# Three more groups of attention scores in float16 pairs, and casts moved from VectorE and ScalarE to GpSimd

## The chip, the cores and the metric

The kernel runs on one core of one Trainium2 chip. A core has a matrix engine (TensorE, PE in the rows, its weight loads PEld), three engines that work on 128 partitions at a time (VectorE DVE, ScalarE ACT, GpSimd POOL) and a queue that issues transfers (SyncE, SP). Each engine works through its own list of instructions in order and waits on semaphores for the others. The metric is the device time of one execution in microseconds (us); less is better.

## The reference

```python
# q, k, v: 8 batches, 12 heads, 448 positions, head size 64, all float32
scores = scale * np.matmul(q, k.transpose(0, 1, 3, 2)) - np.log(S)
attn = 1.0 / (1.0 + np.exp(-scores))
attn_out = np.matmul(attn, v)                       # heads side by side: x is 3584 x 768
gate = 1.0 / (1.0 + np.exp(-(x @ w_gate)))          # w_gate, w_val: 768 x 1536
val = x @ w_val
out = (gate * val) @ w_out                          # w_out: 1536 x 768
```

The weights come as float64 bits of which the kernel makes float32 itself.

## The kernel before, in words

**Attention.** The loop runs over 24 groups m (8 batches times 3 sets of four heads) and, in each, over seven *beats* g, one for each block of 64 keys: 168 beats. In a beat PE computes the scores of that block (L542, in `scores`), ACT applies the sigmoid (L557), and PE multiplies the scores of two beats before with the values (L572). `values` and ACT's copy (L582) give x, which goes to DRAM.

A group's scores are made in one of two ways. In float32, a beat has 8 score matmuls. *In halves* (`in_halves(m)`, before: m odd and from 3 on, eleven groups), each of q and k is split into a high and a low float16 part, and a beat has 12 float16 matmuls. The split is `split_qk(m)`, in three steps. Step one, two groups ahead at beat 0: DVE takes the largest magnitude (L503) and bounds it (L505). Step two, at beat 4: PE sums it over partitions with matmuls behind the next beat's scores (L548), and ACT copies the sum (L559, tile `qka`). Step three, one group ahead at beat 0: DVE makes a power of two (L511, L512), the two high parts (L516), the two low parts (L518) and the factor for the sigmoid (L520, L521). The halves lie in one tile `hl` with one buffer.

**Beside it.** `convert` makes float16 pairs of Strassen-like combinations of the weights, one `step` at a time. For a block of weights (four chunks of 128 x 384, eight steps) DVE takes the magnitude (L216), POOL limits it (L199, `limit`), DVE assembles the float32 (L205, L206, L213) and takes its largest value (L111). Then seven operands: sums of chunks (L261), a cast to the high part (`cast`), DVE's low part (L231, `split`, `lag` steps later) and the store (`send`). During attention the first six blocks (FIRST) are converted, with POOL's casts (L379, `scaled_gpsimd`, one multiplication) and DVE's sums; PACE says which share of the 50 chunk steps is due by which beat. From group 7 on the first x is loaded back (`load_x`), subtracted by DVE (L347, `subtract_x`) and split (`split_x`): a cast (L376 on ACT or L382 on DVE) and DVE's rest (L390), 21 times.

**After attention** come eight visits of the first two layers: each tick is a product of nine matmuls (L719). In the first visit, ticks 2 to 32, the last two blocks of the first part are converted (`in_first` = 2, scales w30 and w31): ACT takes magnitudes (L219), POOL makes the sums (L261), DVE the casts (L382) and the low parts (L231). POOL also multiplies gates with values (L929) and subtracts for the next x (L347). The scale of a block is spread over partitions by one PE matmul (L687) of a tile `each` that DVE makes (L120). The rest of the weights and the output layer follow.

The order on each engine is the order in which the program is written; nothing reorders it.

Of the kernel before, what the change touches and what calls it, by code (L numbers as in the profile page):

```python
# [9 lines left out]
F32 = mybir.dt.float32  # L10
F16 = mybir.dt.float16
# [16 lines left out]
TINY = 2.0 ** -100  # L28
BF16_MAX = 3.3895313892515355e38

PACE = (0, 0), (77, 0.6), (146, 1)

AHEAD, AHEAD_FF = 3, 3

X_LAG, X_BESIDE = 5, 6

SUM_MAX = 2.0 ** 119

# [21 lines left out]
def sigmoid_attention_glu_kernel(ctx: ExitStack, tc: tile.TileContext, qk, v, wg, wv, wo, out):  # L60
# [157 lines left out]
    def magnitude_scalar(to, bits):  # L218
        nc.scalar.activation(to, bits.bitcast(F32), AF.Abs)  # L219

    def convert(words, parts, ks, largest_of, cast, lag, drain_after, adder=nc.gpsimd):

        pool = words.pool

        unsummed, unsplit, unsent, todo, now = [], [], [], {}, 0

        def split():

            while unsplit and unsplit[0][0] + lag <= now:
                _, x, sc, hl, where = unsplit.pop(0)  # L230
                nc.vector.scalar_tensor_tensor(out=hl[:, 1], in0=x, scalar=sc.s, in1=hl[:, 0], op0=ALU.mult, op1=ALU.subtract)  # L231
                unsent.append((hl, where))

        def send():

            while unsent:
                hl, (key, sends) = unsent.pop(0)
                for d in sends(hl):
                    nc.sync.dma_start(**d)
                stored.add(key)  # L240

        def high(x, sc, where):
            hl = pool.tile([P, 2, CW], F16, tag="whl", name="whl", bufs=words.held)
            cast(hl[:, 0], x, sc.s)
            unsplit.append((now, x, sc, hl, where))

        def to_a(jp, t, n):
            return ("a", jp, t, n), lambda hl: [dict(out=a_dram[jp][t][n], in_=hl)]

        def to_op(k, n):  # L250
            return ("o", k, n), lambda hl: [dict(out=o_ops[n][:, :, k, a].rearrange("o p f -> p o f"),
                                                 in_=hl[:, a].rearrange("p (o f) -> p o f", f=P)) for a in range(2)]

        def operands(fs, sc, to):
            a11, a12, a21, a22 = fs
            for x, n in ((a22, 6), (a11, 0), (a12, 4)):
                yield lambda x=x, n=n: high(x, sc, to(n))
            s2 = pool.tile([P, CW], F32, tag="wf4", name="wf", bufs=1)

            def summed(n, x, y, z, op):  # L260
                adder.tensor_tensor(out=x, in0=y, in1=z, op=op)  # L261
# [24 lines left out]
        groups = [(w_scales[jp, t], lambda n, jp=jp, t=t: to_a(jp, t, n), True) for jp, t in parts]
        groups += [(o_scales[k], lambda n, k=k: to_op(k, n), False) for k in ks]
        def value(at, i):
            if at < len(groups) and i < 4:
                value_of[at, i] = pool.tile([P, CW], F32, tag=f"wf{i}", name="wf", bufs=3)  # L290
                words.begin(value_of[at, i])
                return True

        value_of = {}
        for at, (sc, to, everywhere) in enumerate(groups):
            if at == drain_after:
                yield from drain()
            if at in (0, drain_after):
                step(lambda: value(at, 0))
                yield  # L300
                step(words.limit)
                yield
            for i in range(4):
                f = value_of[at, i]
                next_ = (at, i + 1) if i < 3 else (at + 1, 0)
                begun = []

                def first():
                    if next_[1] or next_[0] != drain_after:
# [12 lines left out]
                yield
            fs = [value_of.pop((at, i)) for i in range(4)]
            scale = sc.steps() if everywhere else [sc.row_powers]
            for i, f in enumerate(scale):
                todo.setdefault(now + 1 + i, []).append(f)
            for i, f in enumerate(operands(fs, sc, to)):
                todo.setdefault(now + len(scale) + (0 if everywhere else 1) + i, []).append(f)
        yield from drain()

    def convert_steps(n_groups, everywhere, lag):
        return 8 * n_groups + lag + (TAIL + 4 if everywhere else TAIL)
# [43 lines left out]
        nc.scalar.activation(to, x, AF.Copy, scale=s)  # L376

    def scaled_gpsimd(to, x, s):
        nc.gpsimd.tensor_scalar(out=to, in0=x, scalar1=s, scalar2=None, op0=ALU.mult)  # L379

    def scaled_vector(to, x, s):
        nc.vector.tensor_scalar(out=to, in0=x, scalar1=s, scalar2=None, op0=ALU.mult)  # L382

    casts = itertools.chain((scaled_vector,) * X_BESIDE, itertools.cycle((scaled, scaled_vector)))

    def scaled_in_turn(*args):
        next(casts)(*args)
# [95 lines left out]
    with tc.manual_schedule(), tc.tile_pool(name="att", bufs=2) as att, tc.tile_pool(name="sc", bufs=2, space=PSUM) as scp, \  # L483
# [8 lines left out]
                nc.sync.dma_start(out=loads[m].rearrange("r p t s -> r p (t s)"), in_=qk[m // NQ, m % NQ])  # L492

        def in_halves(m):
            return 1 < m < B * NQ and m % 2 == 1

        def split_qk(m):

            x = loads[m]
            each = att.tile([P, 2], F32, tag="qkm", name="qkm", bufs=1)  # L500
            told = att.tile([P, 2], BF16, tag="qkt", name="qkt", bufs=1)
            total = att.tile([P, 2, 2], F32, tag="qka", name="qka", bufs=1)
            nc.vector.tensor_reduce(out=each, in_=x.rearrange("r p t s -> r t p s"), axis=AX.XY, op=ALU.max,  # L503
                                    apply_absolute_value=True)
            nc.vector.tensor_scalar(out=told, in0=each, scalar1=SUM_MAX, scalar2=TINY, op0=ALU.min, op1=ALU.max)  # L505
# [5 lines left out]
            nc.vector.tensor_tensor(out=m_, in0=total[:, 0], in1=total[:, 1], op=ALU.add)  # L511
            nc.vector.tensor_scalar(out=s_.bitcast(U32), in0=m_.bitcast(U32), scalar1=EXPONENT, scalar2=EXPONENT,  # L512
                                    op0=ALU.bitwise_and, op1=ALU.bitwise_xor)
            hl = att.tile([P, 2, 2, 2, S], F16, tag="hl", name="hl", bufs=1)
            for t in range(2):
                nc.vector.tensor_scalar(out=hl[:, 0, t], in0=x[:, :, t], scalar1=s_[:, t:t + 1], scalar2=None, op0=ALU.mult)  # L516
            for t in range(2):
                nc.vector.scalar_tensor_tensor(out=hl[:, 1, t], in0=x[:, :, t], scalar=s_[:, t:t + 1], in1=hl[:, 0, t],  # L518
                                               op0=ALU.mult, op1=ALU.subtract)
            nc.vector.tensor_scalar(out=inv.bitcast(U32), in0=m_.bitcast(U32), scalar1=EXPONENT, scalar2=None, op0=ALU.bitwise_and)  # L520
            nc.vector.tensor_scalar(out=back, in0=inv[:, 0:1], scalar1=inv[:, 1:2], scalar2=scale / 4, op0=ALU.mult, op1=ALU.mult)  # L521
# [8 lines left out]
        def scores(m, g):  # L530
# [6 lines left out]
            for i, (kt, qt) in enumerate(((1, 0), (0, 1), (0, 0)) if in_halves(m) else ((None, None),)):  # L537
                for h in range(2):
                    for p in range(2):
                        qs, ks_ = (x[halves[h], qt, 0, p], x[halves[h], kt, 1, p, ks]) if in_halves(m) else \  # L540
                            (x[halves[h], p, 0], x[halves[h], p, 1, ks])
                        nc.tensor.matmul(sc[halves[p], h, :S], lhsT=ks_, rhs=qs, start=i == 0, stop=i == 2 or not in_halves(m))  # L542
            sums = qk_sums[:1]
# [64 lines left out]
                                         rhs=bias[halves[h]].to_broadcast([HP, S]), start=True, stop=True)  # L608

        load_first()  # L610
        warm_up(3)
        ones = const.tile([P, HP], BF16, name="ones")
        nc.vector.memset(ones, 2.0 ** (1 - TOP))
        words = Words(att, chunks(halves_of_jps[:FIRST], ()), AHEAD, 6, magnitude_vector)
        weights = convert(words, halves_of_jps[:FIRST], (), max_abs, scaled_gpsimd, 2, None, nc.vector)
        n_chunks, n_weights, done = 8 * FIRST + 2, convert_steps(FIRST, True, 2), 0

        def due_at(beat):
# [442 lines left out]

    in_first = 2 * len(JPS_OF_PARTS[0]) - FIRST
    words = Words(conv, chunks(halves_of_jps[FIRST:], range(KH)), AHEAD_FF, 4, magnitude_scalar)
    weight_casts = itertools.chain((scaled_vector,) * (N_OPS * in_first), itertools.repeat(scaled))
    weights = convert(words, halves_of_jps[FIRST:], range(KH), sum_abs, lambda *args: next(weight_casts)(*args), 1, in_first)
    n_first = convert_steps(in_first, True, 1)
    n_chunks = 8 * (2 * JPS - FIRST - in_first + KH) + 2
    n_all = n_chunks - 2 - 8 * KH + convert_steps(KH, False, 1)
    calm = [t for v_ in range(1, n_a - 1) for t in range(starts[v_] + 2, starts[v_] + 25 if v_ < 3 else starts[v_ + 1] + 2)]
    due = {}  # L1070
    last = n_all - n_chunks
# [51 lines left out]
```

## Time and profile before

| what | us |
|---|---|
| median of 3 runs (lowest, highest) | 1116.47 (1115.51, 1117.61) |
| the profiled execution's own time | 1115.85 |
| its span, first to last instruction | 1113.8 |
| busy: PE, DVE, ACT, POOL | 1103.7, 764.6, 675.7, 427.9 |

The profile's page gives, for each engine, busy time and its share of the span, then forty equal slices of 27.8 us with the busy share in tenths, the chain of work that ended last, and the costliest groups of instructions. A row of the timeline reads: start, length, engine, line, operation, output and inputs, count, and in brackets how long the engine had been idle before it and what ended that wait.

### The profile page before, as it was taken

Reading aid. Unit: us, or ns where it says so; the run is one execution under the profiler, and the core shown is the slowest. Engines: PE = TensorE matmul, PEld = TensorE weight load, DVE = VectorE, ACT = ScalarE, POOL = GpSimd, SP = SyncE. Lnnn points to the kernel's source line nnn. Section 1 sums busy time; section 2 is a strip of 40 time slices with the busy share of each in tenths; the row PEclk is TensorE's granted clock in tenths of the full one; section 3 lists DMA queues with packets and bytes.
Section 4 is the critical chain, followed back from the end, with each engine's and each line's share of the span. In section 5 each row is a group of like instructions: output and inputs, shape, how many; then the busy total and the mean of one; then the engine's idle time right before and its main releaser. Section 6 shows DMA issues by size and latency. Waiting matters only on the chain.

```text
span 1113.8 us, 21314 instructions
## 1 busy us (share of the span) xinstructions
PE 1103.7 (99%) x7642; PEld 556.7 (50%) x7642; DVE 764.6 (69%) x1292; ACT 675.7 (61%) x1278; POOL 427.9 (38%) x371
## 2 busy tenths in 40 slices
PE   9999999999999999999999999999999999999998
PEld 3444444445455555555555555555555555555554
DVE  3769999966974465566567766675339687676863
ACT  6888788887566665866566667665445354253330
POOL 0032323352541342342234433333266193672940
PEclk9999999999999999999999999999999999999999
DMA  8779699779788556843656899898756876867644
GB/s 313 261 237 362 237 311 324 239 268 346 260 283 284 184 177 224 277 125 95 200 176 221 267 360 270 267 288 210 236 156 203 254 229 209 270 202 247 189 127 141
DMA packets 174538, 265.34 MB, mean 238 GB/s; under 512 B 49248, under 2 KB 151264, under 8 KB 174432
## 3 DMA queue, kind: packets, MB, share of 16 engines
q1 hardware_dynamic: 174144, 263.60, 73.4%
q8 instruction: 60, 0.98, 0.4%
q14 instruction: 46, 0.38, 0.1%
q10 hardware_dynamic: 288, 0.38, 0.1%
HBM read 182.48 MB, written 81.43 MB: 237 GB/s over the span
## 4 chain that ended last, share of the span: by engine, by line
PE 93%; DVE 5%; DMA 1%; issue 0%; ACT 0%; DVEq 0%; SPq 0%
PE un L719 76%; PE av L572 9%; PE sc L542 8%; DVE whl L231 1%; DMA wraw<-wv 1%; DVE qkm L503 1%; DVE x0c L111 0%; DVE hl L518 0%; PE sc L607 0%; DVE xt L347 0%; DVE wf L206 0%; DVE hl L516 0%; DVE wf L213 0%; DVE whl L382 0%; DVE wf L205 0%
## 5 line engine op out<-in xcount | busy, mean ns | idle before, releaser
L719 PEld LDWEIGHTS <-A 128*128 128x128 f16 x3024 | 295.5, 98 | 275.8 <-issue 0.7
L719 PE MATMUL un<-b,A 128*128 128x448 f16 x1512 | 296.6, 352 | 0.0
L719 PE MATMUL un<-b,v 128*128 128x448 f16 x1512 | 296.5, 352 | 0.0
L719 PE MATMUL un<-hh,A 128*128 128x448 f16 x1008 | 273.0, 352 | 0.0
L719 PEld LDWEIGHTS <-v 128*128 128x128 f16 x1512 | 147.7, 98 | 137.5
L719 PE MATMUL un<-hl,A 128*128 128x448 f16 x504 | 177.6, 352 | 0.0
L572 PE MATMUL av<-a,v 64*64 64x448 f32 x1344 | 157.2, 538 | 0.0
L199 POOL TENSOR_SCALAR wf<-wf 128x384 f32<-128x384 f32 x72 | 41.9, 582 | 230.4 <-ACT wf L219 126.2
L929 POOL TENSOR_TENSOR g<-c,g 128x448 f32<-128x448 f32 x44 | 59.3, 1348 | 177.9 <-DVE c L702 79.6
L557 ACT ACTIVATE a<-sc,bias 128x896 f32<-128x896 f32 x91 | 91.6, 1008 | 33.2 <-PE sc L542 30.7
L702 DVE TENSOR_TENSOR c<-un,u 128x448 f32<-128x448 f32 x72 | 44.8, 623 | 83.7 <-PE un L719 76.4
L914 ACT ACTIVATE g<-c,back 128x448 f32<-128x448 f32 x72 | 48.1, 668 | 78.9 <-DVE c L702 75.7
L557 ACT ACTIVATE a<-sc,bias,qkb 128x896 f32<-128x896 f32 x77 | 84.9, 1105 | 13.1 <-PE sc L542 6.8
L542 PE MATMUL sc<-qk 64*64 64x448 f32 x728 | 85.0, 536 | 0.3 <-ACT a L557 0.3
L347 POOL TENSOR_TENSOR v<-v 128x448 f32<-128x448 f32 x48 | 64.2, 1366 | 51.1 <-DVE hl L390 50.1
L347 POOL TENSOR_TENSOR b<-b 128x448 f32<-128x448 f32 x48 | 67.5, 1442 | 40.6 <-DVE hl L390 40.6
L572 PEld LDWEIGHTS av<-a,v 64*64 64x64 f32 x1344 | 50.4, 133 | 46.3 <-issue 39.0
L702 DVE TENSOR_TENSOR c<-un,p 128x448 f32<-128x448 f32 x48 | 29.9, 622 | 50.2 <-PE un L719 49.1
L735 ACT COPY p<-un 128x448 f32<-128x448 f32 x48 | 25.5, 532 | 61.6 <-PE un L719 61.5
L542 PE MATMUL sc<-hl 64*64 64x448 f16 x924 | 57.8, 349 | 1.3 <-DVE hl L518 1.3
L347 POOL TENSOR_TENSOR r<-r 128x448 f32<-128x448 f32 x36 | 45.6, 1276 | 30.2 <-DVE b L390 29.9
L261 POOL TENSOR_TENSOR wf<-wf 128x384 f32<-128x384 f32 x48 | 52.8, 1108 | 7.8 <-DVE whl L231 6.6
(359 smaller groups left out, 1409.3 us busy)
## 6 DMA issues: line engine op xcount, KB each, us to landing
A<-ad SPq DMA_DIRECT2D x168, 192.0 KB, 3.4
A<-oo SPq DMA_DIRECT2D x168, 192.0 KB, 2.7
qk<-qk SPq DMA_DIRECT2D x23, 896.0 KB, 7.0
h<-g SPq DMA_DIRECT2D x88, 224.0 KB, 3.4
ad<-whl SPq DMA_DIRECT2D x84, 192.0 KB, 3.2
bd<-b SPq DMA_DIRECT2D x30, 448.0 KB, 4.2
b<-bd SPq DMA_DIRECT2D x30, 448.0 KB, 6.1
v<-vv SPq DMA_DIRECT2D x24, 448.0 KB, 4.2
```

Of the source, the lines that this page charges most:

```text
L199: nc.gpsimd.tensor_scalar(out=f, in0=f, scalar1=F32_MAX, scalar2=F64_ZERO, op0=ALU.min, op1=ALU.max)
L231: nc.vector.scalar_tensor_tensor(out=hl[:, 1], in0=x, scalar=sc.s, in1=hl[:, 0], op0=ALU.mult, op1=ALU.subtract)
L261: adder.tensor_tensor(out=x, in0=y, in1=z, op=op)
L347: engine.tensor_tensor(out=to, in0=x, in1=y, op=ALU.subtract)
L542: nc.tensor.matmul(sc[halves[p], h, :S], lhsT=ks_, rhs=qs, start=i == 0, stop=i == 2 or not in_halves(m))
L557: nc.scalar.activation(a, sc[:, :, :S], AF.Sigmoid, bias=bias, scale=unit)
L572: nc.tensor.matmul(avs[m][p][halves[h], :S], lhsT=vt[halves[p], g, h], rhs=a[halves[p], h], start=g == 0, stop=g == 6)
L702: engine.tensor_tensor(out=to, in0=x, in1=y, op=ALU.add)
L719: nc.tensor.matmul(acc, lhsT=w, rhs=m, start=begin and i == 0, stop=i == len(terms) - 1, skip_group_check=not begin)
L735: nc.scalar.copy(c, acc)
L914: nc.scalar.activation(gates[i], acc, AF.Sigmoid, scale=of_unit[0])
L929: nc.gpsimd.tensor_tensor(out=h, in0=acc, in1=gates[i], op=ALU.mult)
```

## The change

Fourteen groups are made in halves: groups 6, 12 and 18 (ALSO) besides the eleven. The halves are two tiles, high and low, in two sets that even and odd groups use in turn; the even set borrows buffers of x operands. GpSimd's cast is written with two multiplications, the second by 1.0. All 21 casts of the first x go to GpSimd (before: 13 on DVE, 8 on ACT). PACE has 70% of the chunk steps done by beat 77 instead of 60%. In the first visit the 14 casts of w30 and w31 move from DVE to POOL and the 8 sums from POOL to DVE; the low parts there and in all later conversions come two steps behind the casts instead of one. All lines behind L31 have numbers higher by 2, those behind L612 by 4.

```diff
-PACE = (0, 0), (77, 0.6), (146, 1)
+PACE = (0, 0), (77, 0.7), (146, 1)
...
-X_LAG, X_BESIDE = 5, 6
+X_LAG, X_BESIDE = 5, 3 * 7
+
+ALSO = 6, 12, 18
...
-                adder.tensor_tensor(out=x, in0=y, in1=z, op=op)
+                next(adders).tensor_tensor(out=x, in0=y, in1=z, op=op)
...
     def scaled_gpsimd(to, x, s):
-        nc.gpsimd.tensor_scalar(out=to, in0=x, scalar1=s, scalar2=None, op0=ALU.mult)
+        nc.gpsimd.tensor_scalar(out=to, in0=x, scalar1=s, scalar2=1.0, op0=ALU.mult, op1=ALU.mult)
...
-    casts = itertools.chain((scaled_vector,) * X_BESIDE, itertools.cycle((scaled, scaled_vector)))
+    casts = itertools.chain((scaled_gpsimd,) * X_BESIDE, itertools.cycle((scaled, scaled_vector)))
...
         def in_halves(m):
-            return 1 < m < B * NQ and m % 2 == 1
+            return 1 < m < B * NQ and (m % 2 == 1 or m in ALSO)
...
-            told = att.tile([P, 2], BF16, tag="qkt", name="qkt", bufs=1)
-            total = att.tile([P, 2, 2], F32, tag="qka", name="qka", bufs=1)
+            told = att.tile([P, 2], BF16, tag="qkt", name="qkt", bufs=2)
+            total = att.tile([P, 2, 2], F32, tag="qka", name="qka", bufs=2)
...
-            hl = att.tile([P, 2, 2, 2, S], F16, tag="hl", name="hl", bufs=1)
+            hl = halves_of[m % 2]
...
+        halves_of = [[t.rearrange("r (t p) s -> r t p s", t=2) for t in ts] for ts in
+                     ([operand_pairs(at) for at in range(2)], [att.tile([P, 4, S], F16, tag=f"hl{i}", name="hl", bufs=1) for i in range(2)])]
...
-    weight_casts = itertools.chain((scaled_vector,) * (N_OPS * in_first), itertools.repeat(scaled))
-    weights = convert(words, halves_of_jps[FIRST:], range(KH), sum_abs, lambda *args: next(weight_casts)(*args), 1, in_first)
-    n_first = convert_steps(in_first, True, 1)
+    weight_casts = itertools.chain((scaled_gpsimd,) * (N_OPS * in_first), itertools.repeat(scaled))
+    weights = convert(words, halves_of_jps[FIRST:], range(KH), sum_abs, lambda *args: next(weight_casts)(*args), 2, in_first,
+                      itertools.chain((nc.vector,) * (4 * in_first), itertools.repeat(nc.gpsimd)))
+    n_first = convert_steps(in_first, True, 2)
```

DVE's list around groups 11 to 13. Before, the largest value of group 13 (L503) stands among work on x (`xt`, `x0`) and weights (`wf`, `whl`):

```order
L347 TENSOR_TENSOR xt<-u_1363,p_1268 128x448
L503 TENSOR_REDUCE qkm<-qk 128x2
L505 TENSOR_SCALAR qkt<-qkm 128x2
L231 SCALAR_TENSOR_TENSOR whl<-wf,w01s,whl 128x384
L111 TENSOR_REDUCE w11c<-wf 128x1
L216 TENSOR_SCALAR wf<-wraw 128x384
L205 TENSOR_SCALAR wf<-wf 128x384
L206 SCALAR_TENSOR_TENSOR wf<-wraw,wf 128x384
```

Now the third step of group 12 stands ahead of it (`b` is the even set of halves, `qk_2010` the power of two):

```order
L349 TENSOR_TENSOR xt<-u_1487,p_1376 128x448
L513 TENSOR_TENSOR qk_2009<-qka 128x2
L514 TENSOR_SCALAR qk_2010<-qk_2009 128x2
L518 TENSOR_SCALAR b<-qk,qk_2010 128x896 x2
L520 SCALAR_TENSOR_TENSOR b<-qk,qk_2010,b 128x896 x2
L522 TENSOR_SCALAR qk_2011<-qk_2009 128x2
L523 TENSOR_SCALAR qkb<-qk_2011 128x1
L505 TENSOR_REDUCE qkm<-qk 128x2
L507 TENSOR_SCALAR qkt<-qkm 128x2
```

Six instructions (eight, with the pairs) have come in ahead of the reduction of group 13.

POOL's list in the middle of attention, where w10 is cast. Before, it holds weights alone:

```order
L379 TENSOR_SCALAR whl<-wf,w10s 128x384
L199 TENSOR_SCALAR wf<-wf 128x384
L379 TENSOR_SCALAR whl<-wf,w10s 128x384 x2
L199 TENSOR_SCALAR wf<-wf 128x384
L379 TENSOR_SCALAR whl<-wf,w10s 128x384
```

Now casts of x (`b<-p`, `b<-u`, `b<-g`, scale `x0s`) stand between them:

```order
L381 TENSOR_SCALAR whl<-wf,w10s 128x384
L381 TENSOR_SCALAR b<-p_1349,x0s 128x448
L201 TENSOR_SCALAR wf<-wf 128x384
L381 TENSOR_SCALAR whl<-wf,w10s 128x384
L381 TENSOR_SCALAR b<-p_1376,x0s 128x448
L381 TENSOR_SCALAR b<-u_1414,x0s 128x448
L381 TENSOR_SCALAR whl<-wf,w10s 128x384
L381 TENSOR_SCALAR b<-g_1634,x0s 128x448
```

21 such casts have come into POOL's list during attention.

DVE's list in the first visit, from the scale of w30 to the tile `each` of w31, on which PE's matmul L687 waits. Before:

```order
L382 TENSOR_SCALAR whl<-wf,w30s 128x384
L231 SCALAR_TENSOR_TENSOR whl<-wf,w30s,whl 128x384
L382 TENSOR_SCALAR whl<-wf,w30s 128x384
L702 TENSOR_TENSOR c_4406<-un,p_4257 128x448
L231 SCALAR_TENSOR_TENSOR whl<-wf,w30s,whl 128x384
L130 TENSOR_REDUCE w31m<-w31c 128x1
L120 TENSOR_SCALAR each<-w31m 128x128
```

Now:

```order
L706 TENSOR_TENSOR c_4586<-un,p_4436 128x448
L233 SCALAR_TENSOR_TENSOR whl<-wf,w30s,whl 128x384 x2
L263 TENSOR_TENSOR wf<-wf 128x384
L132 TENSOR_REDUCE w31m<-w31c 128x1
L122 TENSOR_SCALAR each<-w31m 128x128
```

The casts have left DVE's list, and a sum of chunks has come into it.

More of the change, by code (lines that the diff above doesn't have):

```diff
@@ L219, in magnitude_scalar, with convert @@
         nc.scalar.activation(to, bits.bitcast(F32), AF.Abs)
-    def convert(words, parts, ks, largest_of, cast, lag, drain_after, adder=nc.gpsimd):
+    def convert(words, parts, ks, largest_of, cast, lag, drain_after, adders=itertools.repeat(nc.gpsimd)):
         pool = words.pool
@@ L513, in split_qk @@
                                     op0=ALU.bitwise_and, op1=ALU.bitwise_xor)
-            hl = att.tile([P, 2, 2, 2, S], F16, tag="hl", name="hl", bufs=1)
+            hl = halves_of[m % 2]
             for t in range(2):
-                nc.vector.tensor_scalar(out=hl[:, 0, t], in0=x[:, :, t], scalar1=s_[:, t:t + 1], scalar2=None, op0=ALU.mult)
+                nc.vector.tensor_scalar(out=hl[0][:, t], in0=x[:, :, t], scalar1=s_[:, t:t + 1], scalar2=None, op0=ALU.mult)
             for t in range(2):
-                nc.vector.scalar_tensor_tensor(out=hl[:, 1, t], in0=x[:, :, t], scalar=s_[:, t:t + 1], in1=hl[:, 0, t],
+                nc.vector.scalar_tensor_tensor(out=hl[1][:, t], in0=x[:, :, t], scalar=s_[:, t:t + 1], in1=hl[0][:, t],
                                                op0=ALU.mult, op1=ALU.subtract)
@@ L539, in scores @@
                     for p in range(2):
-                        qs, ks_ = (x[halves[h], qt, 0, p], x[halves[h], kt, 1, p, ks]) if in_halves(m) else \
+                        qs, ks_ = (x[qt][halves[h], 0, p], x[kt][halves[h], 1, p, ks]) if in_halves(m) else \
                             (x[halves[h], p, 0], x[halves[h], p, 1, ks])
@@ L614, in sigmoid_attention_glu_kernel @@
         words = Words(att, chunks(halves_of_jps[:FIRST], ()), AHEAD, 6, magnitude_vector)
-        weights = convert(words, halves_of_jps[:FIRST], (), max_abs, scaled_gpsimd, 2, None, nc.vector)
+        weights = convert(words, halves_of_jps[:FIRST], (), max_abs, scaled_gpsimd, 2, None, itertools.repeat(nc.vector))
         n_chunks, n_weights, done = 8 * FIRST + 2, convert_steps(FIRST, True, 2), 0
@@ L1063, in sigmoid_attention_glu_kernel @@
     words = Words(conv, chunks(halves_of_jps[FIRST:], range(KH)), AHEAD_FF, 4, magnitude_scalar)
-    weight_casts = itertools.chain((scaled_vector,) * (N_OPS * in_first), itertools.repeat(scaled))
-    weights = convert(words, halves_of_jps[FIRST:], range(KH), sum_abs, lambda *args: next(weight_casts)(*args), 1, in_first)
-    n_first = convert_steps(in_first, True, 1)
+    weight_casts = itertools.chain((scaled_gpsimd,) * (N_OPS * in_first), itertools.repeat(scaled))
+    weights = convert(words, halves_of_jps[FIRST:], range(KH), sum_abs, lambda *args: next(weight_casts)(*args), 2, in_first,
+                      itertools.chain((nc.vector,) * (4 * in_first), itertools.repeat(nc.gpsimd)))
+    n_first = convert_steps(in_first, True, 2)
     n_chunks = 8 * (2 * JPS - FIRST - in_first + KH) + 2
-    n_all = n_chunks - 2 - 8 * KH + convert_steps(KH, False, 1)
+    n_all = n_chunks - 2 - 8 * KH + convert_steps(KH, False, 2)
     calm = [t for v_ in range(1, n_a - 1) for t in range(starts[v_] + 2, starts[v_] + 25 if v_ < 3 else starts[v_ + 1] + 2)]
```

## The prediction

> **What bounds the kernel now.** I read the page first, then the timeline of PE around the scores, then DVE's in the same stretch. Rows carry the line numbers of before.
>
> ```profile
> span 1113.8 us, 21314 instructions
> PE 1103.7 (99%) x7642; PEld 556.7 (50%) x7642; DVE 764.6 (69%) x1292; ACT 675.7 (61%) x1278; POOL 427.9 (38%) x371
> DVE  3769999966974465566567766675339687676863
> ```
>
> PE is busy for 99% of the span, so only less work on PE, or its few waits, can make the kernel faster; and a new wait of PE makes it slower one for one. DVE is at 9 in the slices from the fourth to the eighth, which is 83 to 222 us, in attention. PE's rows there (columns: start, length; the bracket is PE's wait):
>
> ```profile
> 35.76 0.75 PE L542 MATMUL sc<-hl 64*64 64x448 f16 x12
> 37.08 0.75 PE L542 MATMUL sc<-hl 64*64 64x448 f16 x12
> 45.05 0.93 PE L542 MATMUL sc<-qk 64*64 64x448 f32 x8
> 46.56 0.93 PE L542 MATMUL sc<-qk 64*64 64x448 f32 x8
> 55.58 0.75 PE L542 MATMUL sc<-hl 64*64 64x448 f16 x12
> 64.93 0.93 PE L542 MATMUL sc<-qk 64*64 64x448 f32 x8
> 75.45 0.75 PE L542 MATMUL sc<-hl 64*64 64x448 f16 x12
> 118.80 0.22 PE L554 MATMUL sc<-ident,each 64*64 64x64 bf16 x4 [0.21 <-DVE each L120]
> 136.96 0.76 PE L542 MATMUL sc<-hl 64*64 64x448 f16 x12 [1.30 <-DVE hl L518]
> 145.74 0.20 PE L548 MATMUL sc<-qkt,ones 64*64 64x2 bf16 x4 [1.42 <-DVE qkt L505]
> 288.06 0.23 PE L687 MATMUL un<-ident,each 128*128 128x128 bf16 x1 [1.68 <-DVE each L120]
> ```
>
> A beat in halves takes 1.32 us (35.76 to 37.08), one in float32 1.51 (45.05 to 46.56). Group 5, in halves, takes 9.35 us (55.58 to 64.93, its tell matmuls included), group 6, in float32, 10.52 (to 75.45). PE waits for DVE at four places, 0.21 + 1.30 + 1.42 = 2.93 us in attention and 1.68 after it: group 13's halves came too late, and then the largest value of group 15.
>
> How far ahead DVE is before that, its own rows say:
>
> ```profile
> 59.17 0.56 DVE L206 SCALAR_TENSOR_TENSOR wf<-wraw,wf 128x384 uint32<-128x384 uint32 x1
> 64.30 0.16 DVE L511 TENSOR_TENSOR qk<-qka 128x2 f32<-128x2 f32 x1 [3.74 <-ACT qka L559]
> 64.90 1.28 DVE L516 TENSOR_SCALAR hl<-qk,qk 128x896 f16<-128x896 f32 x2
> 66.09 2.21 DVE L518 SCALAR_TENSOR_TENSOR hl<-qk,qk,hl 128x896 f16<-128x896 f32 x2
> 68.55 0.55 DVE L213 SCALAR_TENSOR_TENSOR wf<-wraw,wf 128x384 uint32<-128x384 uint32 x1
> 69.01 0.61 DVE L231 SCALAR_TENSOR_TENSOR whl<-wf,w00s,whl 128x384 f16<-128x384 f32 x1
> 69.54 0.55 DVE L111 TENSOR_REDUCE w01c<-wf 128x1 f32<-128x384 f32 x1
> 70.00 0.36 DVE L216 TENSOR_SCALAR wf<-wraw 128x384 uint32<-128x384 uint32 x1
> 70.29 0.34 DVE L205 TENSOR_SCALAR wf<-wf 128x384 uint32<-128x384 uint32 x1
> 70.67 0.74 DVE L206 SCALAR_TENSOR_TENSOR wf<-wraw,wf 128x384 uint32<-128x384 uint32 x1
> 71.34 0.60 DVE L231 SCALAR_TENSOR_TENSOR whl<-wf,w00s,whl 128x384 f16<-128x384 f32 x1
> 72.34 0.54 DVE L261 TENSOR_TENSOR wf<-wf 128x384 f32<-128x384 f32 x1
> 72.81 0.14 DVE L130 TENSOR_REDUCE w01m<-w01c 128x1 f32<-128x4 f32 x1
> 73.15 2.01 DVE L503 TENSOR_REDUCE qkm<-qk 128x2 f32<-128x1792 f32 x1
> 75.27 0.61 DVE L231 SCALAR_TENSOR_TENSOR whl<-wf,w00s,whl 128x384 f16<-128x384 f32 x1
> 84.12 0.16 DVE L511 TENSOR_TENSOR qk<-qka 128x2 f32<-128x2 f32 x1 [5.06 <-ACT qka L559]
> ```
>
> and a window from the start of group 5's third step (44.74) to the end of group 13's low parts (136.91):
>
> ```profile
> 44.74:136.91 92.17, 79.38 (x171) 1.00 0.83 284
> 132.28 1.85 DVE L516 TENSOR_SCALAR hl<-qk,qk 128x896 f16<-128x896 f32 x2
> 134.05 2.86 DVE L518 SCALAR_TENSOR_TENSOR hl<-qk,qk,hl 128x896 f16<-128x896 f32 x2
> ```
>
> In these 92.17 us DVE worked 79.38 and waited 3.74 and 5.06 for ACT's copy of the sums, which follows PE; behind 84.12 it has no such wait left. So the spare time of DVE, ahead of the place where PE already waits for it, is 8.8 us.
>
> **The change part by part.** *Three groups in halves, on PE.* Each saves 10.52 - 9.35 = 1.17 us, tell matmuls included: 3.5 us in all, if the halves are there in time.
>
> *The same on DVE.* A third step lasts 4.25 us (64.30 to 68.55, next start), a first step 2.12 (73.15 to 75.27): 6.37 us for each group. Groups 6 and 12 fall whole into the window, group 18 behind it.
>
> *PACE, and what follows from it.* The order shows, between the same two points, one more chunk (L111 0.46, L216 0.29, L205 0.38, L206 0.67, L213 0.46, each to the next start: 2.3 us), four more low parts (L231, 0.53 each: 2.1) and two more sums (L261, 0.47 each: 0.9). This work comes later now; group 13 comes too soon for the relief. *x casts off DVE*: the first comes just before group 13, so one of the thirteen lies in the window, at 0.4 us; the others help later, when DVE has no deadline missed.
>
> The sum for DVE's list: 12.7 + 2.3 + 2.1 + 0.9 - 0.4 = 17.6 us more in the window. Without its two waits the window was 92.17 - 8.80 = 83.4 us; with 17.6 it is 101.0. DVE's third step starts 2.1 us behind the start of PE's sixth beat (group 5: 55.58 + 5 x 1.32 = 62.2, and 64.30); for group 6, with PE's float32 scores of group 4, that is 45.05 + 5 x 1.51 + 2.2 = 54.8. DVE stands there at 44.74 + 9.1 (one first and one third step, one chunk, one L213), so it waits 1 us. I take 1 us off again for waits on weight loads that a late DVE no longer meets. Group 13's halves are then ready at 44.74 + 101 = 145.7.
>
> *When PE wants them.* From 55.58: six groups in halves (5, 6, 7, 9, 11, 12) at 9.35 and two in float32 (8, 10) at 10.52 make 77.1, so 132.7. PE waits 13.0 us, somewhere from group 9 on (at the sums of 11 to 13, whose reductions stand in the same queue, or at the halves). Behind a late halves step stand all weight and x work on DVE, and those who wait for them, POOL and the stores, are ahead of need by tens of us; PE is the one that loses. Behind group 13 DVE has 12 casts less (0.45 us each), less weight work, since some came forward, and one group more, so it holds pace and I add nothing. On SP the loads of weights come forward among those of q, k and x; the transfers' share in the window was 0.83, so they still fit, at nothing.
>
> *Casts on GpSimd.* Prices from the groups of instructions:
>
> ```profile
> L199 POOL TENSOR_SCALAR wf<-wf 128x384 f32<-128x384 f32 x72 | 41.9, 582 | 230.4 <-ACT wf L219 126.2 <-DVE wf L216 90.8 <-DMA oo<-whl 5.6
> L379 POOL TENSOR_SCALAR whl<-wf,w10s 128x384 f16<-128x384 f32 x7 | 10.9, 1556 | 17.1 <-DVE w11m L130 6.1 <-DVE wf L261 5.5 <-issue 4.5
> L379 POOL TENSOR_SCALAR whl<-wf,w01s 128x384 f16<-128x384 f32 x7 | 9.3, 1329 | 10.8 <-issue 4.6 <-DVE wf L261 3.2 <-DVE w10m L130 3.0
> L382 DVE TENSOR_SCALAR whl<-wf,w31s 128x384 f16<-128x384 f32 x7 | 6.2, 891 | 0.9 <-POOL wf L261 0.9
> L382 DVE TENSOR_SCALAR whl<-wf,w30s 128x384 f16<-128x384 f32 x7 | 5.3, 753 | 0.0
> L261 POOL TENSOR_TENSOR wf<-wf 128x384 f32<-128x384 f32 x48 | 52.8, 1108 | 7.8 <-DVE whl L231 6.6 <-DVE w31m L130 0.6
> ```
>
> No row shows the form with two multiplications and one scale in memory. L199 has two operations with two constants, 0.58 us; the one-operation cast takes 1.33 to 1.56. I take 0.6, as the form has two operations like L199; the ends are 0.58 and, if the second multiplication is paid on top, twice 1.56 = 3.1. At 0.6 POOL's 42 weight casts fall from some 60 us to 25, and 21 x casts add 14 (0.7 at 448 columns): POOL is far from a bound. At 3.1 it would be one, 63 x 3.1 = 195 us within the 190 us from group 5 on.
>
> *The first visit.* DVE loses 5.3 + 6.2 us of casts and gets 8 sums at 0.54, 4.3 us. PE's wait of 1.68 at 288.06 is for a tile `each` which stood behind three of these casts; I count it as gone. POOL trades 8 x 1.11 = 8.9 us for 14 x 0.6 = 8.4. The second step of lag holds a store back by about a tick (9 matmuls), with SP's operand loads behind it; eight operands are in the ring ahead, so I cost it at nothing, and at 2 us if that cover fails. ACT's eight casts fewer and the later conversions are beside PE: nothing.
>
> *The sum* on the profiled execution: 1115.85 - 3.5 - 2.9 (old waits, which the new one contains) + 13.0 - 1.7 = 1120.8. The median of the runs is 0.6 above that execution, so 1121.4.
>
> *What GpSimd costs DVE.* The pair of L516 and L518 at 132.28 takes 4.63 us, with POOL's casts beside it; the one at 64.90 takes 3.40. So a third step loses at most 1.2 us to POOL, and L206 loses 0.18 (0.74 at 70.67, 0.56 at 59.17). [...]
>
> **The rivals.** *Nearly hidden (about the same).* If DVE ran the window at its lowest prices, twelve L206 at 0.18 less, the dear pair at 1.2 less, and 2% off the other 79 us, 1.6, it would gain 5 us: a wait of 8, 1116.4. For it: shorter casts disturb less. Against it: L206 is disturbed by POOL's limits, which stay, and the third step at 64.90 already ran cheap. It takes a wait under 10.3 to come within 0.2%.
>
> *GpSimd's casts are slow* (1.3 us or more). Then they take tenths of DVE's time in 21 more places and the wait grows by 2 to 5 us; POOL in the first visit is 14 x 1.3 = 18 us for 8.9. Time 1124 to 1128. For it: every scale from memory on POOL in this trace costs 1.3 or more. Against: those have one operation, and L199 with two is twice as fast.
>
> *The other side: DVE gets back what GpSimd took.* If each cast that is 0.75 us shorter gave DVE all of that, the 20 or so weight casts ahead of group 13 would give 15 us, more than the wait of 13, and PE would not wait at all: 1116.5 - 3.5 - 2.9 - 1.7 = 1108.4. It decides for faster (below 1114.2) from 7.2 us given back. Against it: one third step lost 1.2 us at most, and DVE was at work for 79.4 of 92.2 us with most rows near their shortest. [...]
>
> **How the numbers follow.** About 0.2%, 2.2 us, is what a measurement of this kernel can tell from no change. The forecast, a wait of PE of 9 to 17 us, has 0.60 (1117.4 to 1125.4); slow casts 0.13; nearly hidden 0.15; DVE freed 0.12. Time 1121.4. The range from 1115 (nearly hidden is in, DVE freed is out) to 1127 (most of the slow casts) leaves under 2 in 10 out. Slower is 0.60 and 0.13, less 0.03 of the forecast that ends under 1118.7: 0.70. Same takes that and most of nearly hidden: 0.17. Faster is DVE freed and 0.01 of nearly hidden: 0.13.
>
> **What would show it.** Right: in attention PE's rows at L550 or L544 (the tells and scores of the change) for groups 9 to 13 wait for DVE some 10 us or more together, and DVE has no wait for `qka` from group 7 on; attention ends later though 21 more beats last 1.32; the wait at L691 in the first visit is gone; L381 lasts 0.6. Wrong: PE's waits in attention stay under 6 us, because DVE's rows of the window got shorter beside short casts; or the casts last over 1.3 us and POOL is what DVE waits for.

## The result, and the profile after

| what | before | after |
|---|---|---|
| median (lowest to highest), us | 1117.04 (1115.51 to 1118.92) | 1123.97 (1123.83 to 1124.4) |
| ratio, 95% interval | | 1.0062 [1.0044, 1.0079] |
| the profiled execution: own time, span | 1115.85, 1113.8 | 1123.96, 1122.2 |
| end of attention (last score matmul) | 246.5 | 256.45 |

The change makes the kernel slower by 0.6%, 6.9 us. The forecast was 1121.4, with 0.70 for slower.

The page after, its span, busy times, and the slices of PE, DVE and PE's granted clock:

```profile
span 1122.2 us, 21557 instructions
PE 1105.4 (98%) x7738; PEld 562.4 (50%) x7738; DVE 772.6 (69%) x1303; ACT 672.9 (60%) x1273; POOL 425.1 (38%) x398
PE   9999799999999999999999999999999999999998
DVE  3799999983974455566556766675348687676863
PEclk9999899999999999999999999999999999999999
```

PE has a 7 in its fifth slice (112 to 140 us), and there its clock is an 8. The timeline of PE says what stands in it (start, length, and in the bracket the wait). L550, L574, L691 are the lines of the *tell* (the matmuls that sum a group's largest value over partitions), of the products with the values, and of the spread scale in the first visit (before: L548, L572, L687):

```profile
83.29 0.20 PE L550 MATMUL sc<-qkt,ones 64*64 64x2 bf16 x4 [1.01 <-DVE qkt L507]
105.06 0.20 PE L550 MATMUL sc<-qkt,ones 64*64 64x2 bf16 x4 [1.70 <-DVE qkt L507]
119.79 0.22 PE L550 MATMUL sc<-qkt,ones 64*64 64x2 bf16 x4 [4.14 <-DVE qkt L507]
135.23 0.20 PE L550 MATMUL sc<-qkt,ones 64*64 64x2 bf16 x4 [2.99 <-DVE qkt L507]
196.66 0.20 PE L550 MATMUL sc<-qkt,ones 64*64 64x2 bf16 x4 [0.95 <-DVE qkt L507]
119.81 1.79 PE L574 MATMUL av<-a,v 64*64 64x448 f32 x8
126.72 0.94 PE L574 MATMUL av<-a,v 64*64 64x448 f32 x8
296.16 0.22 PE L691 MATMUL un<-ident,each 128*128 128x128 bf16 x1
```

PE waits for the largest values of groups 9, 11, 12, 13 and 19, which DVE brings too late: 10.8 us (10.9 with a gap of 0.13 at 156, ahead of the value of group 15). Behind the wait of 4.14 the same eight matmuls take 1.79 us, three beats later 0.94. The windows show why (columns: window, its length, then busy time and count of PE, PEld, DVE, ACT and POOL, then the granted clock, the share of the transfers and GB/s):

```profile
118.00:120.00 2.00, 0.21 (x8) 0.21 (x11) 1.97 (x3) 0.00 (x0) 0.00 (x0) 0.63 0.00 0
120.00:122.00 2.00, 2.00 (x15) 0.68 (x15) 1.97 (x6) 1.06 (x2) 0.00 (x0) 0.50 0.18 67
122.00:124.00 2.00, 2.00 (x16) 0.77 (x12) 1.90 (x8) 0.78 (x1) 0.63 (x2) 0.50 0.41 150
124.00:126.00 2.00, 2.00 (x24) 1.00 (x20) 1.97 (x6) 0.54 (x2) 1.91 (x3) 0.67 0.01 5
136.00:138.00 2.00, 2.00 (x23) 1.02 (x16) 1.97 (x6) 0.70 (x3) 0.62 (x1) 0.50 0.65 163
138.00:140.00 2.00, 2.00 (x24) 0.82 (x20) 1.90 (x9) 1.18 (x2) 1.01 (x2) 0.75 1.04 401
```

The clock is halved behind the waits of 4.14 and 2.99, which costs PE 2.8 and 1.7 us of work (time below full clock, halved; 0.2 of the 1.7 lies ahead of 136). DVE is at work in every one of these windows.

Which engine sets the time is read from the chain that ended last. Its shares before, then after:

```profile
PE 93%; DVE 5%; DMA 1%; issue 0%; ACT 0%; DVEq 0%; SPq 0%
PE 89%; DVE 9%; DMA 2%; ACT 0%; issue 0%; POOL 0%; DVEq 0%; ACTq 0%; SPq 0%
```

and the chain's pieces in order of time (start, length), here the start and end of its long stretches on DVE, and where it goes back to PE:

```profile
55.87 1.28 DVE b L518 x2
...
153.64 1.94 DVE qkm L505
156.03 0.81 PE av L574 x8
...
177.64 1.28 DVE hl L518 x2
...
190.22 1.81 DVE b L518 x2
192.03 2.12 DVE b L520 x2
194.47 1.94 DVE qkm L505
196.86 0.81 PE av L574 x8
```

From 55.9 to 156 us the chain runs through DVE, and PE's own work and its waits lie beside it. (From 78.9 to 98.4 it names transfers, but no row of DVE there has a wait: DVE was at work all the while.) It runs through DVE again from 177.6 to 196.9, from the third step of group 17 over that of group 18 (tile `b`) to the largest value of group 19. Between the two DVE had caught up: its third step of group 17 waits 1.56 us at 177.16 for the copy of the sums. Behind 196.9 the chain is PE to the end.

### The profile page after: what moved, and what is told of

It reads as the page before. It is cut to its first block, busy times and chain, and to the rows that moved or that the text cites. A ratio compares the mean times of both kernels' runs of the same rounds, so it can differ in the third digit from the quotient of the medians.

```text
span 1122.2 us, 21557 instructions
## 1 busy us (share of the span) xinstructions
PE 1105.4 (98%) x7738; PEld 562.4 (50%) x7738; DVE 772.6 (69%) x1303; ACT 672.9 (60%) x1273; POOL 425.1 (38%) x398
## 4 chain that ended last, share of the span: by engine, by line
PE 89%; DVE 9%; DMA 2%; ACT 0%; issue 0%; POOL 0%; DVEq 0%; ACTq 0%; SPq 0%
PE un L723 76%; PE av L574 6%; PE sc L544 5%; DVE qkm L505 1%; DVE whl L233 1%; DVE hl L520 1%; DMA wraw<-wv 1%; DMA ad<-whl 1%; DVE b L520 1%; DVE wf L208 1%; DVE hl L518 1%; DVE wf L263 1%; DMA xd<-x 0%; DVE x0c L113 0%; PE sc L609 0%; DVE b L518 0%
## 5 line engine op out<-in xcount | busy, mean ns | idle before, releaser
L723 PE MATMUL un<-hl,A 128*128 128x448 f16 x504 | 177.6, 352 | 0.0
L574 PE MATMUL av<-a,v 64*64 64x448 f32 x1344 | 160.6, 547 | 0.0
L559 ACT ACTIVATE a<-sc,bias,qkb 128x896 f32<-128x896 f32 x98 | 108.0, 1105 | 23.7 <-PE sc L550 10.3
L559 ACT ACTIVATE a<-sc,bias 128x896 f32<-128x896 f32 x70 | 70.5, 1008 | 35.1 <-PE sc L544 26.9
L574 PEld LDWEIGHTS av<-a,v 64*64 64x64 f32 x1344 | 51.8, 135 | 37.9 <-issue 29.1
L544 PE MATMUL sc<-qk 64*64 64x448 f32 x560 | 66.4, 544 | 0.4 <-ACT a L559 0.4
L110 ACT ACTIVATE junk<-g 128x448 bf16<-128x448 f32 x88 | 50.5, 574 | 5.3 <-POOL g L933 4.4
```

The lines of the kernel that those rows point to most:

```text
L110: nc.scalar.activation(junk[:, :x.shape[-1]], x, AF.Abs, accum_out=to)
L559: nc.scalar.activation(a, sc[:, :, :S], AF.Sigmoid, bias=bias, scale=unit)
L574: nc.tensor.matmul(avs[m][p][halves[h], :S], lhsT=vt[halves[p], g, h], rhs=a[halves[p], h], start=g == 0, stop=g == 6)
L723: nc.tensor.matmul(acc, lhsT=w, rhs=m, start=begin and i == 0, stop=i == len(terms) - 1, skip_group_check=not begin)
```

## The experiments

The theory: DVE's list in attention got longer than PE's time, so PE waits; what is taken out of DVE's list ahead of PE's last wait for it comes back, and nothing else does. The rivals: single waits, or the halved clock behind them, are what costs; or GpSimd's casts hold DVE up. Diffs are against the changed kernel unless it is said otherwise.

**1. Without group 12.**

```diff
-ALSO = 6, 12, 18
+ALSO = 6, 18
```

> The changed kernel with group 12 back in float32 (groups 6 and 18 stay in halves); all else as changed. Theory (DVE's list ahead of group 13 is too long): the list loses one first and one third step, 6.4 us, so PE's lateness at the tell of group 13 falls from 13.3 us to about 7; one wait of about 4 us in place of waits of 4.14 and 2.99, perhaps with a slow clock behind it. Against before: two groups gain 2.4, the old waits 2.9 and 1.7 go, 7 to 10 come: +0 to +3 us, so 4 to 7 us less than the changed kernel. Rival (GpSimd's many casts slow DVE): group 12 matters only by its own 1.2 us, the time stays within 2 us of the changed kernel.

Measured 1117.36, ratio to before 1.0002 [0.9994, 1.0011]: 6.6 us less than after. PE's waits for DVE sum to 7.8 us, the longest is 2.86, and the clock stays full. One group of 6.4 us of DVE's work, which saves PE 1.17, is worth 6.6 us. The theory holds.

**2. The two long waits filled with work.** PE repeats the scores of one beat 6 times (group 10) and of another 11 times (group 11), just ahead of the two long waits, so that it stays busy.

```diff
+AGAIN = {(10, 5): 6, (11, 5): 11}
...
-            for i, (kt, qt) in enumerate(((1, 0), (0, 1), (0, 0)) if in_halves(m) else ((None, None),)):
+            for i, (kt, qt) in enumerate((((1, 0), (0, 1), (0, 0)) if in_halves(m) else ((None, None),)) * AGAIN.get((m, g), 1)):
+                i = i % 3 if in_halves(m) else 0
```

> The changed kernel, in which PE makes the scores of two beats again while it would wait: those of group 10, beat 5, six times in all and those of group 11, beat 5, eleven times (5 x 0.75 and 10 x 0.57 us more work, the same result). If the slow clock comes from PE standing still, the granted clock stays at 1.0 in 115 to 140 us. Theory (DVE sets when PE goes on at the tell of group 13, so slowness before that point is covered): only what was lost behind the last wait comes back, 1.7 us. Rival (all the slow clock is lost): 4.5 us come back. Second rival (the clock falls for another reason): nothing comes back and the clock is 0.5 there as before.

Measured 1124.04, ratio 1.0061 [1.0048, 1.0073]: the same as after. Its windows of 60 us, and PE's waits (lines two higher here):

```profile
60.00:120.00 60.00, 56.88 (x772) 27.49 (x768) 58.22 (x121) 44.88 (x55) 15.64 (x22) 1.00 0.88 309
120.00:180.00 60.00, 58.21 (x867) 28.75 (x861) 56.01 (x115) 44.68 (x55) 21.19 (x27) 1.00 0.76 258
154.99 0.20 PE L552 MATMUL sc<-qkt,ones 64*64 64x2 bf16 x4 [1.20 <-DVE qkt L508]
```

The same windows of after:

```profile
60.00:120.00 60.00, 53.15 (x736) 25.94 (x732) 58.22 (x119) 45.04 (x55) 15.64 (x22) 0.99 0.88 311
120.00:180.00 60.00, 56.88 (x743) 28.34 (x743) 56.01 (x116) 44.72 (x54) 21.19 (x27) 0.93 0.74 253
```

The clock stays at 1.00, and nothing comes back: DVE's busy time is the same to the hundredth (58.22 and 56.01), and what PE gained it spends in other waits (0.59 at 125.3, where after has none, and 1.20 at 154.99, where after has 0.13). The repeats, 5 x 0.75 + 10 x 0.57 = 9.45 us, and the waits that are left (1.02, 1.72, 0.38, 0.59, 1.20, 0.95) make 15.3 us; waits and halved clock make 15.4 in after. Both expectations that gave something back for the clock missed, and so did the second rival, by which the clock would have stayed at 0.50: the halved clock lay beside DVE's list. This is the plainest sign that DVE set the pace.

**3. One multiplication in GpSimd's cast.**

```diff
-scalar2=1.0, op0=ALU.mult, op1=ALU.mult)
+scalar2=None, op0=ALU.mult)
```

> The changed kernel with GpSimd's cast by one multiplication, as before. The casts then last 1.25 to 1.5 us instead of 0.6 to 1.0. Theory: DVE's list is what counts; it loses some tenths beside each longer cast, 1 to 3 us more waiting ahead of group 13, and POOL's list in the first visit gets about 7 us longer: +1 to +4 us against the changed kernel. Rival (the two multiplications are what made it slow): the time falls by 2 us or more.

Measured 1128.98, ratio 1.0104 [1.0087, 1.012]: 5.0 us slower than after, more than expected. POOL's casts in attention (window to 262 us, POOL's busy time and count of this line alone, then clock, transfers and GB/s), here and then in after:

```profile
0.00:262.00 262.00, 100.19 (x63) 0.97 0.77 266
```

```profile
0.00:262.00 262.00, 54.81 (x63) 0.98 0.79 273
```

and the low parts of groups 13 and 23 on DVE, here and then in after:

```profile
146.88 2.58 DVE L520 SCALAR_TENSOR_TENSOR hl<-qk,qk,hl 128x896 f16<-128x896 f32 x2
247.05 2.85 DVE L520 SCALAR_TENSOR_TENSOR hl<-qk,qk,hl 128x896 f16<-128x896 f32 x2
```

```profile
144.46 2.19 DVE L520 SCALAR_TENSOR_TENSOR hl<-qk,qk,hl 128x896 f16<-128x896 f32 x2
241.00 2.52 DVE L520 SCALAR_TENSOR_TENSOR hl<-qk,qk,hl 128x896 f16<-128x896 f32 x2
```

DVE's list is the same in both, instruction by instruction. Up to the end of group 23's low parts POOL's casts take 43.4 us more (93.99 for 50.62, 59 casts), and DVE is 2.4 us late at group 13 and 6.0 at group 23, about a seventh. In the same 410 instructions DVE is busy 214.09 us for 210.46: 3.6 us of it are longer instructions, a twelfth of 43.4. The rest is waits; DVE waits 2.9 us instead of 1.1 for casts of x on POOL. (The profiled execution of this run, 1130.81, is the slowest of its four.)

By the prediction's third rival, in which DVE gets back all that the casts are shorter by, DVE would have lost up to the 43 us here. The loss is there, and is far smaller (6.0 us late at group 23); what causes it is not shown.

**4. The two multiplications alone**, in the kernel before.

```diff
-scalar2=None, op0=ALU.mult)
+scalar2=1.0, op0=ALU.mult, op1=ALU.mult)
```

> The kernel before, with GpSimd's cast written with two multiplications and nothing else. The run with one multiplication showed VectorE's list, the same 1303 instructions, 2.4 us later at the halves of group 13 and 5 us later at its end of attention. Theory (VectorE gets back about a tenth of what the casts lose; 42 casts of 1.3 to 1.6 us become 0.6 to 0.9): VectorE reaches group 13's halves 1 to 2 us earlier, PE's waits of 2.93 us in attention fall by 1.3 to 2.7, and the one of 1.68 in the first visit stays: 1114 to 1115.3. Rival (the cast's length does not matter while GpSimd is not the bound): 1116 to 1117.

Measured 1115.44 against 1115.77, ratio 0.9992 [0.9982, 1.0001]: nothing that can be told from no change. The 42 casts fall from 60.96 to 33.70 us, and the wait ahead of group 13's halves from 1.30 to 0.97; the next one (1.42, now 1.43) stays. The expected 1.3 us did not come. Ahead of group 13 POOL's casts fall by only 11 us (23.17 to 12.02), and DVE's busy time in the window 44.74 to 136.91 falls from 79.38 to 78.09; why no more of that reaches PE is not shown.

**5. The three groups alone**, in the kernel before: double buffers and ALSO, with no cast, PACE or first visit changed.

```diff
+ALSO = 6, 12, 18
...
-            return 1 < m < B * NQ and m % 2 == 1
+            return 1 < m < B * NQ and (m % 2 == 1 or m in ALSO)
...
-            hl = att.tile([P, 2, 2, 2, S], F16, tag="hl", name="hl", bufs=1)
+            hl = halves_of[m % 2]
...
```

> The kernel before with the three more groups in halves and their double buffers alone: PACE, the casts, the sums and the first visit as before. Theory (two more halves steps ahead of group 13 are the larger part of what overfills DVE's list: 12.7 of 17.6 us): PE waits 11 to 14 us in attention for 2.9 before, less 3.5 of beats, the wait of 1.7 in the first visit stays, and 0 to 2 for the slow clock: 5 to 9 us slower than before. Rival (the moved weight work and the casts do it, the groups by themselves gain): 0 to 3 us faster than before.

Measured 1126.3 against 1116.26, ratio 1.0087 [1.0072, 1.0103]: 10.0 us slower, a little above what was expected. In attention PE waits 2.65, 1.61, 2.99, 1.49, 1.52 and 1.47 for DVE; and in the first visit there is

```profile
298.59 0.29 PE L691 MATMUL un<-ident,each 128*128 128x128 bf16 x1 [3.14 <-DVE each L122]
```

which was 1.68 before and is gone in after: the first-visit exchange does what it was counted for.

**6. All of the change but the groups.**

```diff
-PACE = (0, 0), (77, 0.7), (146, 1)
+PACE = (0, 0), (77, 0.6), (146, 1)
...
-ALSO = 6, 12, 18
+ALSO = ()
```

> The changed kernel with no new group in halves and PACE as before: what is left is the casts with two multiplications, all of x's casts on GpSimd, and the first visit's casts and sums exchanged. Theory: DVE is disturbed less, PE's waits in attention fall from 2.9 us to 1 to 1.5, the wait of 1.7 in the first visit is gone: 3 us less than before, 1113.5 to 1114.5. Rival (the moved casts bring no time): 1116 to 1118.

Measured 1113.01, ratio 0.997 [0.996, 0.9981]: 3.25 us faster. PE's waits in attention are 0.72 and 1.14 (before 2.93 in all), and that of 1.68 is gone: 2.75 of it. So the three groups with their PACE turn a gain of 3.3 into a loss of 6.9.

**7. The three groups with the pace of before** (60% by beat 77, end at 146).

```diff
-PACE = (0, 0), (77, 0.7), (146, 1)
+PACE = (0, 0), (77, 0.6), (146, 1)
```

> The changed kernel with 60% of the chunk steps done by beat 77, as before, and the end at beat 146 kept. By beat 84 (the third step of group 13) 4.5 chunk steps fewer are due than in the changed kernel, by beat 117 (the largest value of group 18) 2.1 fewer. Theory (VectorE's list sets the pace up to the last wait at 195.7 us, so only what is taken out ahead of that counts): PE's waits ahead of group 13 shrink by about 5 us, others behind it take half of that back, and the time is 1121 to 1122.5. Rival (group 13 decides, as the prediction's sum has it): all 5.3 us come back, 1118 to 1119.5.

Measured 1121.62, ratio 1.0047 [1.0033, 1.0061]: 2.35 us less than after (1.7 by the two ratios to before, as before took 0.6 us less beside this run), as the theory had it. PE's waits:

```profile
115.27 0.20 PE L550 MATMUL sc<-qkt,ones 64*64 64x2 bf16 x4 [2.65 <-DVE qkt L507]
142.02 0.76 PE L544 MATMUL sc<-hl 64*64 64x448 f16 x12 [2.58 <-DVE hl L520]
193.22 0.20 PE L550 MATMUL sc<-qkt,ones 64*64 64x2 bf16 x4 [1.63 <-DVE qkt L507]
```

Up to group 13 they sum, with 1.14 at 127.9, to 6.37 (after: 9.84); behind it, with 0.58 at 181.9 and 0.90 at 212.9, to 3.11 (after: 1.08). Work moved past group 13 comes back at groups 18 to 21.

**8. Group 6 alone, groups 6 and 18**, both with a later end of the conversion.

```diff
-PACE = (0, 0), (77, 0.7), (146, 1)
+PACE = (0, 0), (77, 0.6), (150, 1)
...
-ALSO = 6, 12, 18
+ALSO = 6,
```

> The changed kernel with group 6 alone added, PACE at 60% by beat 77 and all by beat 150. Theory: group 6's 6.4 us fit into the 8.8 us that DVE had to spare ahead of group 9, and every deadline behind it is met: 1.2 for the group, 2.9 and 1.7 for the old waits: 5.8 us less than before, less up to 1.5 for small waits: 1111 to 1113. Rival (the weight work that is left for the end holds up the first operands of the first visit, as with PACE ending at 160): 1114 to 1118, with a wait of PE in the first visit.

> The same with groups 6 and 18. Theory: 1.2 us less again, but a wait of up to 1 at the tell of group 19: 1110.5 to 1113. Rival: as for the run with group 6, 1114 to 1118, the first visit later still since DVE's list ends later.

Group 6 alone: 1109.99 against 1116.26, ratio 0.9942 [0.993, 0.9955], better than both kernels, by a little more than expected. The chain of its page is 99% PE, and behind the first beats one wait over 0.4 us is left in PE's rows, 1.59 at 120.0 for a tile `each`.

Against run 6 the median falls by 3.0 us, and the end of PACE differs too (150, not 146). The group gives 1.17 and the waits 0.3; where the other 1.5 is from stays open. The two profiled executions differ by only 0.57 (1112.35 for run 6, and here 1111.78, the slowest of six): the group and the waits, less a first beat 0.72 later (5.50 for 4.78), are as much as that, to 0.2.

Groups 6 and 18: 1115.74, ratio 0.9995 [0.9986, 1.0003]. The theory missed; the rival's time came, at another place than the rival said:

```profile
185.56 0.22 PE L550 MATMUL sc<-qkt,ones 64*64 64x2 bf16 x4 [4.33 <-DVE qkt L507]
```

That is the largest value of group 19, behind the third step of group 18 on DVE.

**9. Groups 6 and 18 with half of the steps by beat 77 and the end at 160.**

```diff
-PACE = (0, 0), (77, 0.7), (146, 1)
+PACE = (0, 0), (77, 0.5), (160, 1)
...
-ALSO = 6, 12, 18
+ALSO = 6, 18
```

> The changed kernel with groups 6 and 18 alone added and PACE at 50% by beat 77 and all by beat 160. Theory: DVE's list meets every deadline, PE waits at most 1 us in attention, the clock stays at 1.0: against before 2 x 1.2 + 2.9 + 1.7 = 7.0 us less, less up to 1: 1110 to 1111.5. Rival (new waits appear elsewhere, or the first visit starts later as more weight work lies at the end of attention): 1113 to 1117.

Measured 1118.38, ratio 1.0007 [0.9996, 1.0018]: a miss. Attention ends at 245.43, 11 us sooner than after, but late weight work holds up the first visit, and PE pays there:

```profile
260.50 2.02 PE L723 MATMUL un<-b,A 128*128 128x448 f16 x5 [4.20 <-ACT u L739]
```

The chain says how: eight stores of converted weights, the last of which waits for DVE's last low part, stand in SP's queue from 249.2 to 255.6; the next weights (`wraw` from `wg`) are asked for behind them at 255.66; ACT waits 7.57 us for these to take their magnitude (L221); and the copy of `u`, for which PE waits, stands behind that in ACT's list.

**10. Late groups instead**: 22, or 20 and 22, with group 6, at the pace of run 8 (first diff; the second has `6, 20, 22`).

```diff
-PACE = (0, 0), (77, 0.7), (146, 1)
+PACE = (0, 0), (77, 0.6), (150, 1)
...
-ALSO = 6, 12, 18
+ALSO = 6, 22
```

> Groups 6 and 22 in halves with the pace of the version with group 6 alone (60% by beat 77, end at 150), which took 1109.99. There the halves of 21 and 23 are ready 6.7 and 7.3 us ahead of PE. Theory (an added group costs nothing where VectorE is 6.4 us or more ahead, and gives 1.17): 1108.3 to 1109.4, no new wait. Rival (as with group 18: a largest value comes late, PE waits 4 us): 1111 to 1114.

> The same with group 20 as well. In the version with group 6 alone the halves of 19 are ready 6.1 us ahead of PE, those of 17 4.9. Theory: one more group of 6.4 us about uses the lead up, waits of 0 to 1 us, 1107.5 to 1109. Rival (the lead is used up at the largest values of 19 to 21, as group 18 did): a wait of 2 to 4 us, 1110 to 1113.

1113.34, ratio 0.9972 [0.9963, 0.998], and 1119.53, ratio 1.0027 [1.0017, 1.0037]. The theory missed both, by 3.9 and 10.5 us; with 22 the rival's time came, and with 20 and 22 the waits of its kind were three. With 22 PE has a second wait, 1.79 at 258.7, which comes as in run 9 (ACT waits 5.17 us for `wraw` there); its profiled execution, 1115.27, is the slowest of eleven. Besides the wait near 120 that run 8 has too, PE's waits in attention for a largest value, with 22, then with 20 and 22:

```profile
225.93 0.20 PE L550 MATMUL sc<-qkt,ones 64*64 64x2 bf16 x4 [1.80 <-DVE qkt L507]
```

```profile
206.24 0.20 PE L550 MATMUL sc<-qkt,ones 64*64 64x2 bf16 x4 [3.00 <-DVE qkt L507]
218.43 0.22 PE L550 MATMUL sc<-qkt,ones 64*64 64x2 bf16 x4 [2.70 <-DVE qkt L507]
231.89 0.22 PE L550 MATMUL sc<-qkt,ones 64*64 64x2 bf16 x4 [2.48 <-DVE qkt L507]
```

A lead of 6 us at the halves was the wrong sign to go by. The deadline that falls first is the next group's largest value, which DVE makes behind the third step of the added group, and it is due five beats after it. Between two groups in halves that follow each other DVE has 6.4 us of work for 9.35 of PE, with all weights and x in what is left.

## Why the prediction was right, and where it was off

**The mechanism was right.** PE waits for DVE from group 9 on, at the values of 9, 11, 12 and 13, within the groups 9 to 13 that the prediction named. From group 7's third step (69.81) up to group 13 and beyond, DVE waits for `qka` no more; only at group 17 it does, 1.56 us. Its window holds more work, 88.14 us in 181 instructions (the third pair below; before 79.38 in 171):

```profile
69.81 0.45 DVE L513 TENSOR_TENSOR qk<-qka 128x2 f32<-128x2 f32 x1
44.74:136.91 92.17, 82.33 (x1080) 39.17 (x1073) 88.14 (x181) 66.78 (x84) 20.35 (x29) 0.96 0.78 272
```

Group 13's halves were forecast for 145.7 and are done at 146.65 (144.46 + 2.19, above). The third step of group 5, from which the sum counts, starts at 45.39 instead of 44.74, so its 101.0 us became 101.3. The lateness forecast as 13.0 us is 12.6 at group 13's value: waits of 9.84 and 2.8 of halved clock. Leaving group 12 out (run 1) gives back its price.

**Groups in halves, −3.5**: 3.1. PE's busy time in attention is 239.64 us, less 4.5 of halved clock 235.1, for 238.25 before; group 6 alone (run 8) has 237.14 for 238.27 in run 6, which is 1.13 of the 1.17. **The old waits contained**: as forecast, the waits of before are in the list above no more.

**The first visit, −1.7**: right, by the L691 row above, and by its growth to 3.14 where the exchange is missing (run 5).

**PACE, 5.3 of the 13.0**: the size ahead of group 13 is about right (3.5 us of waits less in run 7, and about 1 of halved clock), but it is no cost of its own: 2.0 us of it come back as waits later, and the time moves by 2.35.

**Behind group 13, "I add nothing": wrong.** This is the step that failed. The lateness grows on: 1.7 of halved clock and 0.13 by 156 us, 0.95 at 196.7, so 15.4 (with the 12.6) instead of 13.0 in all. The halved clock is no cause there (run 2). The chain shows the cause: DVE's list runs on to group 15's value, and again from 177.6 to that of group 19, with the third step of group 18 in it. As DVE had caught up at 177.16, the 0.95 is group 18's own price, and not left over from group 13. The casts that I set against group 18 lie partly behind that place (at least three of the twelve: before, they stood at 205 to 224 us). This makes 2.4 us of the 3.2 by which the sum for the profiled execution (1120.8) is short of its 1123.96. Another 0.5 is a later start (first beat at 5.50, before 5.03, in run 1 4.79), in which executions scatter, and 0.4 the groups' 3.1 in place of 3.5; that closes the sum to 0.1.

**Casts on GpSimd, 0.6 us**: too low. The shortest take 0.58, as L199 does, but the mean of the 63 in attention is 0.87 (54.81 us above), 0.78 to 0.98 for weights and 0.72 to 0.99 for x, as here:

```profile
L381 POOL TENSOR_SCALAR whl<-wf,w01s 128x384 f16<-128x384 f32 x7 | 5.4, 776 | 13.5 <-DVE wf L263 5.5 <-issue 5.4 <-DVE w10m L132 2.5
```

**The rivals.** "GpSimd's casts are slow" did not come, as the casts are short; but its price was right: with long casts the time is 1129 (run 3), 5.0 more, at the upper end of its 2 to 5 (and over its 1124 to 1128, since the time that it adds to is 2.6 over my sum). "DVE gets back what GpSimd took" had the right sign and at most a seventh of the size (run 3: 6.0 of 43.4 us), and in the kernel before no gain that can be told from none (run 4). That all of it comes back was my assumption; no run shows it. "Nearly hidden" had DVE's rows shorter; group 13's halves came 1 us later than my sum, not sooner.

## What to carry to other kernels

Where a helper engine makes operands for a bound engine, a faster form on the bound engine is worth something only up to the point at which the helper's list is full: here one added group of 6.4 us on VectorE, at a slightly later pace, gave 3 us against run 6 (1.5 of which stay unexplained), and two or three gave nothing or cost up to 11, at several paces. In a kernel of this kind, look for the first deadline in the helper's list behind the added work (here the next group's largest value), not for the lead of the added product itself. And sum a lateness up to the last place where the helper is waited for, since relief that is only moved in time returns as the next wait.

## What the runs showed of the hardware

**The granted clock of TensorE after a wait.** It falls to 0.50 late in some waits of 2.5 to 4.3 us or at their end (4.33 is that of groups 6 and 18 in run 8), and not by length alone: the wait of 2.86 in run 1 and that of 3.00 in run 10 left it at 1.00, while 2.65 in run 7, and 2.70 and 2.48 in run 10, halved it. The windows of run 7 behind 2.65:

```profile
115.00:116.00 1.00, 0.73 (x8) 0.32 (x11) 0.96 (x4) 0.43 (x1) 0.00 (x0) 0.67 0.07 25
116.00:117.00 1.00, 1.00 (x12) 0.48 (x8) 1.00 (x4) 0.63 (x2) 0.00 (x0) 0.50 0.05 16
117.00:118.00 1.00, 1.00 (x11) 0.36 (x8) 0.97 (x3) 0.00 (x0) 0.55 (x1) 0.50 0.88 240
118.00:119.00 1.00, 1.00 (x12) 0.38 (x8) 1.00 (x4) 0.34 (x1) 0.41 (x1) 0.62 0.54 165
```

The time at 0.50 in these four is 0.66 + 1 + 1 + 0.76 = 3.4 us; about the wait of 4.14 in after (from 118.5, within the wait) it is 1.5 + 2 + 2 + 1.3 = 6.8, twice that. The same sum over such windows gives 3.4 us for 2.99 in after, 2.65, 2.99 and 3.14 in run 5, 2.58 in run 7, 4.33 in run 8, and 2.70 and 2.48 in run 10, and 6.8 for 4.20 in run 9. Why waits of like length differ, these runs do not show.

**A multiplication by 1.0 makes GpSimd's cast shorter**: 128 x 384 from float32 to float16 with a scale in memory takes 1.24 us at least with one multiplication (before and run 3), 0.58 at least with two (after); the 42 casts of run 4 took 33.70 us instead of 60.96.
